# PSUM arrays of one bank each, late exponentials per bank, weight sums after batch 1, earlier attention ranks in a fused attention and MLP kernel

## The chip, the cores and the metric

The kernel runs on one core of a Trainium2 chip. The metric is the device time of one execution in microseconds (us); the time of a kernel is the median of its runs. Before the change it is 321.23 us, the median of three runs (321.04 to 321.79).

The engines are named as in the profile: PE is the matrix engine (PEld its weight loads, which overlap its matmuls), DVE the vector engine, ACT the scalar engine, POOL the GpSimd engine, SP the queue that issues nearly all DMA transfers. Each engine works through its own list of instructions in order; semaphores hold an instruction until what it depends on is done. PE writes its results to PSUM, which has eight banks of 512 fp32 columns on 128 partitions; ACT and DVE read them there.

## The reference

Two stages: windowed attention for eight heads, then an MLP with a leaky ReLU.

```python
# q, k, v: (8 batches, 8 heads, 576 positions, 64), float32
scores = (1 / sqrt(64)) * q @ k.T                        # per batch and head
rel = pos[:, None] - pos[None, :]
mask_plain = (rel >= 0) & (rel < 32)                     # heads 0 to 3
mask_dil = (rel >= 0) & (rel < 128) & (rel % 4 == 0)     # heads 4 to 7
scores = where(mask, scores, -1e9)
attn = exp(scores - max); attn = attn / (sum(attn) + 1e-9)
x = (attn @ v) -> (4608 tokens, 512)                     # heads side by side
h = x @ w_in                                             # 512 -> 2048
g = maximum(0.01 * h, h)
out = g @ w_out                                          # 2048 -> 512, float32
```

## The kernel before

**Work.** Operands are cast to fp16 on the chip. Attention is cut into windows: a block of 96 queries needs 128 keys, and the dilated heads become plain ones when positions are taken modulo 4. Heads go in pairs (`hp`): 0 and 1 are plain (group `g` = 0), 2 and 3 dilated (`g` = 1). Batches 0 and 1 ("early") go through `unit` (L726), three units for each pair, the third one in a second part with its own load (`load_rest`); batches 2 to 7 ("late") go through `late_unit` (L862), two units for each pair, eight for each batch. The attention output is put, transposed, into one of two buffers `xt` (one for each pair of batches). The MLP then works on chunks of 384 tokens, three for each pair of batches, twelve in all: `up` (L994) makes 16 blocks of the hidden layer for a chunk, each four matmuls into a bank `hps` and one ACT eviction with the leaky ReLU into `gt` (L1022). Chunk 0 needs batch 0, chunk 1 batch 1, chunk 2 the rest of both, chunk 3 batch 2, chunk 4 batch 3, chunk 5 the rest of these, and so on (the last three chunks come in the order batch 6, rest, batch 7). The first eight tiles of 128 tokens get their down-projection in the plain way (`down`, L1052: 16 matmuls of 512 columns into a bank `fps`, in four parts, evicted by DVE at L1071 and stored). The other 28 tiles go in groups of four through `group` (L1102), which makes the product of 2 x 2 blocks with seven block products (L1150) in place of eight, and for this needs sums of blocks of `w_out`.

**One attention unit.** The chain is: PE makes transposed q and k for a pair of heads (early: transposes L611 into bank `tpf`, copied out by DVE or ACT at L563 or L561 into `slots`; late: DVE transposes L593 and L604, with POOL's copies L598). PE makes the scores (early L757 or L771, for some units after a bias matmul L754; late L893 or L900). ACT takes the exponential (early L777, late L908). DVE masks (early L791, late L922). PE multiplies with the values, with a column or block of ones for the row sums (early L803, L815, L825, L835; late L929). Early units get the reciprocal on ACT as Ln (L847) and Exp (L849) and are normalised by DVE (L853); late units use DVE's reciprocal (L947) and normalisation (L951), and `across` (L960) transposes the result on PE (L977) and copies it to `xt` (L561 on ACT or L563 on DVE).

**PSUM.** Line 238 makes two arrays of two banks each: `s_two`, with `sps0` (scores of early units) and `tpf` (transposes) as its halves, and `o_two`, with the two `ops` banks as its halves. A late unit writes its scores to both halves of `s_two`, and one exponential of 576 columns reads both. Successive units take the two `ops` banks in turn. `hps0`, `hps1`, `fps0` and `fps1` are arrays of one bank each. In the last group the halves of both arrays serve as four more output banks.

**Weight sums.** `weight_sums` (L1088) makes four DVE instructions of 2048 columns (L1092). Sums 1, 2 and 4 wait for all of `w_out` to be cast, sum 3, written in place, also for the plain down-projections.

**Order.** The order on every engine is fixed when the program is built. `_Plan.run` (L85) goes through all tasks with estimated durations and, where several tasks are ready for an engine, takes the one with the lowest rank (`prio`). The MLP blocks have ranks of `begins[c] + j * 1.3` with `begins` in steps of 20.8 for each chunk. The attention of batch b from 2 on gets ranks from `WHEN[b - 1]` to `WHEN[b]`; batches 0 and 1 have `RANKS`. Loads and casts have ranks from a counter of their own (`tick`), stores come before all. The weight sums have rank `SUMS` = 75. Where the plan leaves PE idle, short matmuls on zeros (L1358) fill in. The plan knows the data and buffer dependencies that the code names; the waits in the program itself come from the accesses to each array and are put in by the framework.

Of the kernel before, what the change touches and what calls it, by code (L numbers as in the profile page):

```python
# [10 lines left out]
FP32 = mybir.dt.float32  # L11
AF = mybir.ActivationFunctionType
# [1 line left out]

WIN = 32
AHEAD, LATE = 5.0, 4.0
WHEN = (-5.0, 15.0, 50.0, 77.0, 112.0, 138.0, 172.0, 200.0)
CON = -1484.5
LOCK = 60.0
AFTER = -1495.0  # L20
# [41 lines left out]
class _Plan:  # L62
# [5 lines left out]
    def add(self, eng, dur, lat, deps, fn, prio, soft=0.0, kind=""):  # L68
        choices = eng if isinstance(eng, tuple) else ((eng, dur),)
        t = _Task(choices, lat, deps, fn, prio, soft, len(self.tasks), kind)  # L70
        self.tasks.append(t)
        return t
# [70 lines left out]
def kernel(  # L143
# [10 lines left out]
    nc = tc.nc  # L154
# [10 lines left out]
    SCALE = float(1.0 / np.sqrt(D))  # L165
# [11 lines left out]
    ps = ctx.enter_context(tc.tile_pool(name="ps", bufs=1, space=bass.MemoryType.PSUM))  # L177
# [4 lines left out]
    def bank(name, dt=FP32):  # L182
        return ps.tile([128, 512 if dt == FP32 else 1024], dt, name=name)

    def at(tl, p0, p1, off, *dims):

        row = tl.ap[0][0]
        return bass.AP(tensor=tl.tensor, offset=tl.offset + p0 * row + off,
                       ap=[[row, p1 - p0]] + [list(d) for d in dims])
# [45 lines left out]
    wide = wst[0].bitcast(FP16)  # L235
    sums = {1: wide[:, 0:2048], 2: wide[:, 2048:4096], 4: t4}

    s_two, o_two = (ps.tile([128, 1024], FP32, name=n) for n in ("sps", "ops"))
    sps0, tpf = s_two[:, 0:512], s_two[:, 512:1024]
    tpb = tpf.bitcast(FP16)  # L240
    ops = [o_two[:, 512 * i:512 * i + 512] for i in range(2)]
    hps = [bank(f"hps{i}") for i in range(2)]
    banks = {"S": [sps0], "O": ops}
    banks["S0"] = banks["S"] + hps[1:]
# [5 lines left out]
    add = plan.add  # L250
# [243 lines left out]
    w_used = [[] for _ in range(16)]  # L494
# [367 lines left out]
    def late_unit(b, g, i, n, prio, turned):  # L862

        dil = g == 1
        hp = 2 * g + i
        ready, t_users, qb, kb = turned[hp]
        _, _, _, vt, v_deps, v_users = visits[b, hp, 0]
        if "S2" not in rings:
            rings["S2"] = [rings["S"][-1] + rings["TP"][-1]]
            o = rings["O"]  # L870
            rings["O2"] = [next(o[-k] for k in (1, 2) if (len(o) - k) % 2 == x) for x in range(2)]
            rings["ED"] = [[] for _ in range(NL)]
            rings["EP"] = [sum(rings["E"][-NE:], [])] * 2
            rings["XN"] = [sum(rings["R"][-NR:], [])] * 2
            rings["REC"] = [[] for _ in range(4)]
        _, s_old = ring("S2", 1, s_users := [])
        en, e_old = ring("ED" if dil else "EP", NL if dil else 2, e_users := [])
        on, o_old = ring("O2", 2, o_users := [])
        cn, c_old = ring("REC", 4, c_users := [])
        if i == 0 and n == 0:  # L880
            xn, x_old = ring("XN", 2, x_users := [])
            xnat[b, g] = x_nat[xn], x_old, x_users, []
        xb, x_old, x_users, made = xnat[b, g]
        et, ot, rt = (el if dil else ee2)[en], ops[on], rec[cn]
        dims = [[192, 2], [336, 2], [1, 144]] if dil else [[1, 576]]
        s_dims = [[512, 2], [144, 2], [1, 144]] if dil else [[512, 2], [1, 288]]

        def scores(e):
            for y in range(2):
                if dil:  # L890
                    c = 2 * n + y
                    for w, k0, c0, x in ((96, 0, 0, 48 * y), (48, 64, 96, 96 * (1 - y))):
                        nc.tensor.matmul(at(s_two, 0, 128, 512 * y + x, [144, 2], [1, w]),  # L893
                                         at(kb, 0, 128, PAD + c + k0, [4, 128]),
                                         at(qb, 0, 128, c * 144 + c0, [S, 2], [1, w]),
                                         start=True, stop=True)
                    continue
                for x in range(3):
                    t = 3 * n + x
                    nc.tensor.matmul(s_two[:, 512 * y + 96 * x:512 * y + 96 * x + 96],  # L900
                                     at(kb, 0, 128, 96 * t, [1, 128]),
                                     at(qb, 0, 128, y * S + 96 * t, [1, 96]),
                                     start=True, stop=True)

        t_s = add("PE", 0.25, 0.25, ready + s_old, scores, prio + 0.1, 0.4, "s")
        t_users.append(t_s)
        t_e = add("ACT", 0.06 + 576 * 0.00085, 0.22, [t_s] + e_old + t_gap,
                  lambda e: nc.scalar.activation(out=at(et, 0, 128, 0, *dims),  # L908
                                                 in_=at(s_two, 0, 128, 0, *s_dims),
                                                 func=AF.Exp, scale=SCALE), prio + 0.1)  # L910
        s_users.append(t_e)

        def mask(e):
            io = [[288, 2], [1, 288]]
            if dil:
                mk, io = at(con, 0, 128, M_DIL, [144, 2], [0, 2], [1, 144]), dims
            elif n == 0:
                mk = at(con, 0, 128, M_PL, [0, 2], [1, 288])
            else:
                mk, io = at(con, 0, 128, M_PL + 96, [0, 6], [1, 96]), [[96, 6], [1, 96]]  # L920
            x = at(et, 0, 128, 0, *io)
            nc.vector.tensor_tensor(out=x, in0=x, in1=mk, op=ALU.mult)  # L922

        t_m = add("DVE", 0.08 + 576 * 0.00056, 0.15, [t_e, t_con], mask, prio + 0.1, 0.0, "M")

        def values(e):
            def one(t, hh, c, k, first, last):
                r = 65 * (2 * t + hh)
                nc.tensor.matmul(ot[:, r:r + 65], et[:, c:c + 128],  # L929
                                 at(vt, 0, 128, (hh * (8 if dil else 6) + k) * 128, [1, 65]),  # L930
                                 start=first, stop=last)
            for t in range(3):
                for hh in range(2):
                    if not dil:
                        one(t, hh, 288 * hh + 96 * t, 3 * n + t, True, True)
                    elif t < 2:
                        one(t, hh, 336 * hh + 240 * t, 2 * n + t, True, True)
                    else:
                        one(t, hh, 336 * hh + 96, 4 + 2 * n, True, False)
                        one(t, hh, 336 * hh + 144, 5 + 2 * n, False, True)  # L940

        t_v = add("PE", 0.23 if dil else 0.17, 0.25, [t_m] + v_deps + o_old, values, prio + 0.2,
                  0.4, "v")
        e_users.append(t_v)
        v_users.append(t_v)
        t_r = add("DVE", 0.13, 0.15, [t_v] + c_old,
                  lambda e: nc.vector.reciprocal(out=rt[0:96, :], in_=at(ot, 0, 96, 64, [65, 6])),  # L947
                  prio + 0.2)

        def norm(e):  # L950
            nc.vector.tensor_tensor(  # L951
                out=at(xb, 0, 96, 768 * n + 64 * i, [256, 3], [128, 2], [1, D]),
                in0=at(ot, 0, 96, 0, [130, 3], [65, 2], [1, D]),
                in1=at(rt, 0, 96, 0, [2, 3], [1, 2], [0, D]), op=ALU.mult)
        t_n = add("DVE", 0.1 + 384 * 0.0011, 0.2, [t_r] + x_old, norm, prio + 0.2)
        o_users.append(t_n)
        c_users.append(t_n)
        made.append(t_n)

    def across(b, g, prio):  # L960
# [3 lines left out]
        for i in range(2):  # L964
# [19 lines left out]
            for c in (chunk_at(m, S * (b % 2)), chunk_at(m, 384)):  # L984
                x_done.setdefault((c, 0), []).append(t_x)

    xnat = {}
    x_nat = [t.bitcast(FP16) for t in rc2]
    t_gap = [clear("POOL", at(t, 0, 128, 144, [336, 2], [1, 48]), 0.15, 0.0, -600) for t in el]
# [90 lines left out]
    def w_block(k, n):  # L1080
        return at(w_out, 0, 128, k * HJ * DM + n * HN, [DM, HJ], [1, HN])

    def flat(tl):
        return at(tl, 0, 128, 0, [HN, HJ], [1, HN])
# [3 lines left out]
    def weight_sums():  # L1088
        w_all = sum((w_out_t[j] for j in range(NJ)), [])

        def minus(n, dst, x, y, deps):
            t_sum[n] = add("DVE", 1.2, 0.2, deps, lambda e: nc.vector.tensor_tensor(  # L1092
                out=dst, in0=x, in1=y, op=ALU.subtract), SUMS, 0.0, "T")
        minus(1, flat(sums[1]), w_block(0, 1), w_block(0, 0), w_all + w_used[9] + w_used[10])
        minus(2, flat(sums[2]), w_block(1, 1), flat(sums[1]), [t_sum[1]])
        minus(4, flat(sums[4]), w_block(1, 0), flat(sums[2]), [t_sum[2]] + rings["VST"][-1])
        minus(3, w_block(0, 1), w_block(1, 1), w_block(0, 1), [t_sum[1]] + plain_parts)
# [265 lines left out]
    for t, u in zip(pe, pe[1:]):  # L1363
# [4 lines left out]
        x = t.start + t.dur + 0.1  # L1368
# [43 lines left out]
```

## Time and profile before

| what | value |
|---|---|
| runs | 321.79, 321.23, 321.04 us |
| the profiled execution's own time | 321.56 us |
| its span, from first to last instruction | 319.8 us |
| busy: PE / PEld / DVE / ACT / POOL | 300.6 / 215.5 / 201.6 / 175.7 / 122.8 us |
| granted PE clock | 1.00 |
| first matmul of chunk 1's up-projection after its wait | 64.88 us |
| weight sums 1, 2 and 4 (L1092) start at | 55.55, 57.88 and 61.62 us, and take 1.22 us each |
| batches 2 to 7: last copy into `xt` ends | 101.8, 130.7, 164.3, 190.1, 234.7, 260.1 us |
| chunks 3, 4, 6, 7, 9, 10 (the first that need these): first eviction starts | 109.3, 131.4, 171.0, 195.5, 245.6, 263.9 us |
| last matmul ends | 315.6 us |

Busy time is the union of an engine's instructions. A matmul's end is modelled: matmuls follow each other faster than their rows are long (a row of 128x384 columns shows 326 ns, eight of them stand in 1.30 us on the chain of waits). So a PE that is busy all the time in this profile may still have short gaps, and idle time in it is surely idle. The two rows on batches and chunks are from the timeline: 24 copies of 576 columns into `xt`, four for each late batch, and sixteen evictions for each chunk (32 in chunk 2, which is cut in halves), counted in order of time.

### The profile page before, as it was taken

The page shows a single profiled execution, that of the slowest core. Times are in us where ns is not written, and L with a number is a line of the kernel's source. Part 1 is how long each engine was busy: PE and PEld are TensorE (multiplying, and loading weights), DVE is VectorE, ACT ScalarE, POOL GpSimd, SP SyncE. Part 2 cuts the span into 40 slices and gives each one's busy share as a digit, 9 for nine tenths or more (in the row PEclk, how much of TensorE's full clock was granted, in tenths as well). Part 3 has the DMA queues.
Part 4 walks back from the last instruction along what each step waited for, and adds up shares of the span by engine and source line. Part 5 has one row for each costly group of instructions (what it writes and reads, how often), then busy time and mean ns, then how long its engine had stood idle before and what let it go on. Part 6 is the DMA issues. An engine that isn't in the chain of part 4 may idle for free.

```text
span 319.8 us, 7327 instructions
## 1 busy us (share of the span) xinstructions
PE 300.6 (94%) x2796; PEld 215.5 (67%) x2796; DVE 201.6 (63%) x421; ACT 175.7 (55%) x376; POOL 122.8 (38%) x178
## 2 busy tenths in 40 slices
PE   7786977899999997999999999999999999999994
PEld 3543643456777765778777877877877777777883
DVE  5754677964774669968989669768744542151342
ACT  3635753586665564645676546466446645455320
POOL 4459554083836457616772955556000000000000
PEclk9999999999999999999999999999999999999999
DMA  7999999699599998697899969794103010210033
GB/s 248 311 336 401 400 306 157 153 229 199 99 238 190 165 230 164 131 188 150 159 210 228 167 138 182 190 187 113 35 10 92 2 33 2 61 49 25 26 107 101
DMA packets 163187, 51.25 MB, mean 160 GB/s; under 512 B 140752, under 2 KB 160080, under 8 KB 163152
## 3 DMA queue, kind: packets, MB, share of 16 engines
q1 hardware_dynamic: 162128, 50.05, 66.0%
q10 hardware_dynamic: 1024, 0.73, 0.8%
q8 instruction: 22, 0.36, 0.5%
q14 instruction: 13, 0.11, 0.1%
HBM read 41.32 MB, written 9.44 MB: 159 GB/s over the span
## 4 chain that ended last, share of the span: by engine, by line
PE 82%; DVE 8%; ACT 5%; issue 1%; DVEq 0%; ACTq 0%
PE hps L1011 36%; PE fps L1150 24%; PE fps L1063 6%; PE ops L929 3%; DVE slots L563 3%; PE ops L977 2%; PE sps L900 2%; PE sps L893 2%; DVE xt L853 1%; ACT ee L777 1%; ACT gt L1022 1%; PE ops L1150 1%; DVE ee L922 1%; ACT rc L847 1%; PE sps L754 1%
## 5 line engine op out<-in xcount | busy, mean ns | idle before, releaser
L1011 PE MATMUL hps<-xt,w_in 128*128 128x384 f16 (+1 forms) x812 | 145.4, 313 | 1.6 <-DVE xt L853 0.6
L1022 ACT ACTIVATE gt<-hps 128x384 f16<-128x384 f32 (+1 forms) x203 | 94.1, 467 | 74.7 <-PE hps L1011 71.6
L1011 PEld LDWEIGHTS <-w_in 128*128 128x128 f16 x832 | 75.9, 98 | 38.0 <-issue 2.0
L1150 PEld LDWEIGHTS <-gt 128*128 128x128 f16 x672 | 64.5, 98 | 11.9
L598 POOL COPY slots<-turned 64x576 f16<-64x576 f16 x48 | 35.9, 747 | 59.5 <-DVE turned L593 48.0
L1150 PE MATMUL fps<-w_out,gt 128*128 128x256 f16 x416 | 53.6, 273 | 0.0
L274 POOL CAST nat<-stg 128x576 f16<-128x576 f32 (+1 forms) x53 | 37.2, 727 | 8.1 <-DMA stg<-in_q_dram 5.2
L1063 PE MATMUL fps<-w_out,gt 128*128 128x512 f16 x128 | 32.7, 379 | 0.2 <-DVE osb L1071 0.2
L1187 DVE TENSOR_TENSOR osb<-fps,stg 128x512 f32<-128x512 f32 x18 | 12.3, 683 | 24.6 <-ACT stg L1179 18.4
L951 DVE TENSOR_TENSOR rc<-ops,recs 96x384 f16<-96x384 f32 x48 | 25.9, 543 | 1.2 <-PE ops L929 0.6
L563 DVE COPY slots<-sps 64x128 f16<-64x128 f16 (+7 forms) x43 | 13.6, 334 | 13.3 <-PE sps L611 6.7
L1179 ACT COPY stg<-fps 128x512 f32<-128x512 f32 (+1 forms) x24 | 12.8, 533 | 14.5 <-PE fps L1150 13.1
L947 DVE RECIPROCAL recs<-ops 96x6 f32<-96x6 f32 x48 | 8.7, 183 | 19.0 <-PE ops L929 18.7
L922 DVE TENSOR_TENSOR ee<-ee,con 128x576 f16<-128x576 f16 x24 | 16.8, 699 | 5.9 <-ACT ee L908 5.6
L274 POOL CAST vd<-v_all 128x1024 f16<-128x1024 f32 (+2 forms) x20 | 17.2, 876 | 6.3 <-DMA v_all<-in_v_dram 5.3
L908 ACT ACTIVATE ee<-sps 128x576 f16<-128x576 f32 x24 | 15.6, 650 | 5.9 <-PE sps L900 5.0
L1063 PEld LDWEIGHTS <-gt 128*128 128x128 f16 x128 | 11.7, 98 | 9.8 <-issue 0.6
L604 DVE STREAM_TRANSPOSE slots<-nat 128x576 f16<-128x576 f16 x24 | 17.8, 748 | 0.6 <-POOL nat L274 0.6
L908 ACT ACTIVATE el<-sps 128x576 f16<-128x576 f32 x24 | 15.6, 650 | 4.5 <-PE sps L893 3.7
L593 DVE STREAM_TRANSPOSE turned<-nat 128x576 f16<-128x576 f16 x24 | 18.0, 755 | 0.0
L922 DVE TENSOR_TENSOR el<-el,con 128x576 f16<-128x576 f16 x24 | 12.8, 535 | 7.6 <-ACT el L908 7.5
L777 ACT ACTIVATE ee<-sps 128x384 f16<-128x384 f32 x20 | 9.8, 490 | 13.0 <-PE sps L771 4.8
(112 smaller groups left out, 378.9 us busy)
## 6 DMA issues: line engine op xcount, KB each, us to landing
stg<-in_q_dram SPq DMA_DIRECT2D x48, 144.0 KB, 3.4
stg<-in_k_dram SPq DMA_DIRECT2D x48, 144.0 KB, 2.9
v_all<-in_v_dram SPq DMA_DIRECT2D x24, 256.0 KB, 4.3
v_all<-in_v_dram SPq DMA_DIRECT2D x24, 192.0 KB, 3.2
gt<-in_moe_w_in_dram SPq DMA_DIRECT2D x5, 512.0 KB, 7.9
out_dram<-osb SPq DMA_DIRECT2D x24, 96.0 KB, 2.0
out_dram<-osb SPq DMA_DIRECT2D x36, 48.0 KB, 1.7
out_dram<-osb SPq DMA_DIRECT2D x25, 64.0 KB, 2.1
```

The source lines that it names most:

```text
L274: ENG[e].tensor_copy(out=dst, in_=src)
L563: nc.vector.tensor_copy(out=dst, in_=src)
L593: lambda e: nc.vector.transpose(xb, na[:, 0:S]), prio)
L598: lambda e, p0=p0, hh=hh: nc.gpsimd.tensor_copy(out=at(qb, p0, p0 + 64, hh * S + o, *od), in_=at(xb, p0, p0 + 64, i, *id_)), prio, 0.0, "m ...
L604: lambda e: nc.vector.transpose(kb[:, PAD:PAD + S], na[:, S:2 * S]), prio)
L908: lambda e: nc.scalar.activation(out=at(et, 0, 128, 0, *dims), in_=at(s_two, 0, 128, 0, *s_dims), func=AF.Exp, scale=SCALE), prio + 0.1)
L922: nc.vector.tensor_tensor(out=x, in0=x, in1=mk, op=ALU.mult)
L951: nc.vector.tensor_tensor(out=at(xb, 0, 96, 768 * n + 64 * i, [256, 3], [128, 2], [1, D]), in0=at(ot, 0, 96, 0, [130, 3], [65, 2], [1, D]) ...
L1011: nc.tensor.matmul(ht[:, 0:n], at(w_in, 0, 128, i * DFF + j // 2 * 256 + j % 2, [2, 128]), at(xt[m % 2], 0, 128, i * 1152 + x0, *dims), st ...
L1022: lambda e: nc.scalar.activation(out=gt[c % NG][:, j * n_c + x:j * n_c + x + n], in_=ht[:, 0:n], func=AF.Prelu, alpha=0.01),
L1063: nc.tensor.matmul(ft, g[:, j * n_c + tt * 128:j * n_c + tt * 128 + 128], w_out[:, j * DM:j * DM + DM], start=(j == 0), stop=(j == NJ - 1))
L1150: nc.tensor.matmul(bk[:, x:x + HN], tl[:, off + j * step:off + j * step + 128], rhs(j), start=first and x == 0 and j == 0, stop=j == HJ - ...
```

## The change

The two arrays of two banks become four arrays of one bank (`bank("sps0")`, `bank("tp")`, `bank("ops0")`, `bank("ops1")`). Since one instruction can no longer read both score banks, a late unit has two exponentials of 288 columns, one for each bank, in place of one of 576, and its mask waits for both. The first weight sum now also waits for the last normalisations of batch 1's second part (`x_done[2, 1]`); sums 2 and 4 follow it. `WHEN`, the ranks of the late batches' attention, gets smaller numbers from its third entry on. Nothing that is computed changes.

```diff
--- before.py
+++ after.py
@@ -14,7 +14,7 @@
 
 WIN = 32
 AHEAD, LATE = 5.0, 4.0
-WHEN = (-5.0, 15.0, 50.0, 77.0, 112.0, 138.0, 172.0, 200.0)
+WHEN = (-5.0, 15.0, 46.0, 70.0, 100.0, 126.0, 160.0, 188.0)
 CON = -1484.5
 LOCK = 60.0
 AFTER = -1495.0
@@ -235,10 +235,9 @@
     wide = wst[0].bitcast(FP16)
     sums = {1: wide[:, 0:2048], 2: wide[:, 2048:4096], 4: t4}
 
-    s_two, o_two = (ps.tile([128, 1024], FP32, name=n) for n in ("sps", "ops"))
-    sps0, tpf = s_two[:, 0:512], s_two[:, 512:1024]
+    sps0, tpf = bank("sps0"), bank("tp")
     tpb = tpf.bitcast(FP16)
-    ops = [o_two[:, 512 * i:512 * i + 512] for i in range(2)]
+    ops = [bank(f"ops{i}") for i in range(2)]
     hps = [bank(f"hps{i}") for i in range(2)]
     banks = {"S": [sps0], "O": ops}
     banks["S0"] = banks["S"] + hps[1:]
@@ -883,32 +882,35 @@
         xb, x_old, x_users, made = xnat[b, g]
         et, ot, rt = (el if dil else ee2)[en], ops[on], rec[cn]
         dims = [[192, 2], [336, 2], [1, 144]] if dil else [[1, 576]]
-        s_dims = [[512, 2], [144, 2], [1, 144]] if dil else [[512, 2], [1, 288]]
 
         def scores(e):
             for y in range(2):
                 if dil:
                     c = 2 * n + y
                     for w, k0, c0, x in ((96, 0, 0, 48 * y), (48, 64, 96, 96 * (1 - y))):
-                        nc.tensor.matmul(at(s_two, 0, 128, 512 * y + x, [144, 2], [1, w]),
+                        nc.tensor.matmul(at(s_two[y], 0, 128, x, [144, 2], [1, w]),
                                          at(kb, 0, 128, PAD + c + k0, [4, 128]),
                                          at(qb, 0, 128, c * 144 + c0, [S, 2], [1, w]),
                                          start=True, stop=True)
                     continue
                 for x in range(3):
                     t = 3 * n + x
-                    nc.tensor.matmul(s_two[:, 512 * y + 96 * x:512 * y + 96 * x + 96],
+                    nc.tensor.matmul(s_two[y][:, 96 * x:96 * x + 96],
                                      at(kb, 0, 128, 96 * t, [1, 128]),
                                      at(qb, 0, 128, y * S + 96 * t, [1, 96]),
                                      start=True, stop=True)
 
         t_s = add("PE", 0.25, 0.25, ready + s_old, scores, prio + 0.1, 0.4, "s")
         t_users.append(t_s)
-        t_e = add("ACT", 0.06 + 576 * 0.00085, 0.22, [t_s] + e_old + t_gap,
-                  lambda e: nc.scalar.activation(out=at(et, 0, 128, 0, *dims),
-                                                 in_=at(s_two, 0, 128, 0, *s_dims),
-                                                 func=AF.Exp, scale=SCALE), prio + 0.1)
-        s_users.append(t_e)
+        t_e = []
+        for y in range(2):
+            def exps(e, y=y):
+                o = (at(et, 0, 128, 192 * y, [336, 2], [1, 144]) if dil
+                     else et[:, 288 * y:288 * y + 288])
+                nc.scalar.activation(out=o, in_=s_two[y][:, 0:288], func=AF.Exp, scale=SCALE)
+            t_e.append(add("ACT", 0.06 + 288 * 0.00085, 0.22, [t_s] + e_old + t_gap, exps,
+                           prio + 0.1))
+        s_users += t_e
 
         def mask(e):
             io = [[288, 2], [1, 288]]
@@ -921,7 +923,7 @@
             x = at(et, 0, 128, 0, *io)
             nc.vector.tensor_tensor(out=x, in0=x, in1=mk, op=ALU.mult)
 
-        t_m = add("DVE", 0.08 + 576 * 0.00056, 0.15, [t_e, t_con], mask, prio + 0.1, 0.0, "M")
+        t_m = add("DVE", 0.08 + 576 * 0.00056, 0.15, t_e + [t_con], mask, prio + 0.1, 0.0, "M")
 
         def values(e):
             def one(t, hh, c, k, first, last):
@@ -984,6 +986,7 @@
             for c in (chunk_at(m, S * (b % 2)), chunk_at(m, 384)):
                 x_done.setdefault((c, 0), []).append(t_x)
 
+    s_two = (sps0, tpf)
     xnat = {}
     x_nat = [t.bitcast(FP16) for t in rc2]
     t_gap = [clear("POOL", at(t, 0, 128, 144, [336, 2], [1, 48]), 0.15, 0.0, -600) for t in el]
@@ -1091,7 +1094,7 @@
         def minus(n, dst, x, y, deps):
             t_sum[n] = add("DVE", 1.2, 0.2, deps, lambda e: nc.vector.tensor_tensor(
                 out=dst, in0=x, in1=y, op=ALU.subtract), SUMS, 0.0, "T")
-        minus(1, flat(sums[1]), w_block(0, 1), w_block(0, 0), w_all + w_used[9] + w_used[10])
+        minus(1, flat(sums[1]), w_block(0, 1), w_block(0, 0), w_all + w_used[9] + w_used[10] + x_done[2, 1])
         minus(2, flat(sums[2]), w_block(1, 1), flat(sums[1]), [t_sum[1]])
         minus(4, flat(sums[4]), w_block(1, 0), flat(sums[2]), [t_sum[2]] + rings["VST"][-1])
         minus(3, w_block(0, 1), w_block(1, 1), w_block(0, 1), [t_sum[1]] + plain_parts)
```

## The prediction

> **What bounds the kernel now.** I read the busy time by stretches first, then the waits and the chain of waits of the stretches where TensorE (PE) is not full, then the timeline there. By stretches, columns being length, PE, PE weight loads, DVE, ACT, POOL, clock, DMA share and GB/s:
>
> ```profile
> 36.00:66.00 30.00, 24.70 (x216) 13.36 (x214) 24.95 (x63) 16.49 (x41) 12.47 (x17) 1.00 0.88 240
> 66.00:120.00 54.00, 53.79 (x538) 37.30 (x537) 34.12 (x74) 35.31 (x83) 29.64 (x40) 1.00 0.95 188
> 120.00:128.00 8.00, 5.89 (x59) 4.38 (x58) 7.43 (x11) 3.81 (x8) 5.78 (x8) 1.00 0.87 165
> 128.00:316.00 188.00, 187.41 (x1772) 144.55 (x1769) 115.06 (x215) 101.70 (x202) 54.65 (x71) 1.00 0.50 108
> ```
>
> From 66 us on PE idles 0.2 us up to 120, 2.1 us from 120 to 128 and 0.6 us up to 316, and the granted clock is full. The change takes no matmul of the projections away, so nearly all that it can win is PE idle time: the 2.1 us, and the 5.3 us (30.00 less 24.70) of 36 to 66, where batch 1's attention has to end before chunk 1's up-projection can start at 64.88. Before 36 us there is more idle time, but the first up-projections wait there for weights: POOL's cast of the fourth w_in tile at 22.59 sat 2.45 us for its DMA, and the DMA share of 20 to 40 us is 1.05.
>
> The timeline of 36 to 66 shows what the waits are (start, length, instruction, idle time before it and what ended it):
>
> ```profile
> 46.39 0.49 ACT L777 ACTIVATE ee<-sps 128x384 f16<-128x384 f32 x1 [0.38 <-DVE slots L563]
> ...
> 46.92 0.41 DVE L563 COPY slots<-sps 64x480 f16<-64x480 f16 x1 [0.56 <-ACT ee L777]
> ...
> 51.62 0.28 PE L815 MATMUL ops<-ee,vd 128*64 128x96 f16 x4 [0.93 <-DVE xt L853]
> ```
>
> The exponential reads bank sps0. The copies of L563 read transposed q and k in the other bank of the same array, tpf. Neither needs the other's data, yet each waits for the other, two reads in turn. L815 likewise writes the ops bank whose last reader ended at 50.43, but starts when the reader of the other ops bank ends, at 51.57. Arrays of one bank don't do this: from 77.72 ACT reads one hps array while PE writes the other without a gap (76.87 to 78.33). So the program orders by array, and the change does what it says.
>
> **Part 1, four arrays.** PE's waits in 36 to 66:
>
> ```profile
> PE ops L815 <- DVE xt L853: 0.9, 1, 0.9
> PE sps L754 <- DVE slots L563: 0.7, 1, 0.7
> PE hps L1011 <- DVE xt L853: 0.6, 1, 0.6
> PE ops L835 <- ACT rc L847: 0.6, 1, 0.6
> PE ops L815 <- ACT rc L847: 0.5, 1, 0.5
> PE ops L835 <- DVE xt L853: 0.5, 1, 0.5
> ```
>
> All but the L1011 row are of the cross-bank kind: 0.9 + 0.7 + 0.6 + 0.5 + 0.5 = 3.2 us. A 384-column matmul has a row of 326 ns but follows its like every 162 ns (8 in 1.30 us), so each gap is understated by some 0.16 us: 5 x 0.16 = 0.8, together 4.0 us. What stands behind them: for the L835 and L815 rows the reader of their own bank had ended 0.5 to 1.2 us before, so these go whole if their other inputs are there; L754 is followed at once by L771, which needs the copies, so that one only shrinks as the copies stop waiting for the exponential (0.61 us at 42.56). PE then reaches the next attention step sooner, and some of those will not be ready. I take a third off: 2.7 us, bounds 1.3 and 6.9 (5.3 plus ten gaps of 0.16, all idle time gone). DVE, at 83% in this stretch, is next in line; without the sums below it has 24.95 less 3.65 = 21.3 us of work there, so it allows 6 us or more.
>
> In 26 to 36 the waits of L757 are 1.1 (on slots) and 0.8 us (on an exponential that had itself sat 2.94 us behind copies of the other bank). But POOL's casts at 35.19 and 36.47 wait 0.77 and 0.67 us for DMA, which sets the pace anew. I take 0.3 us, bounds 0 and 1.9.
>
> In 120 to 128:
>
> ```profile
> 122.11 3.14 DVE L922 TENSOR_TENSOR ee<-ee,con 128x576 f16<-128x576 f16 x1
> ...
> 126.50 0.34 PE L929 MATMUL ops<-vp,ee 128*128 128x65 f16 x6 [2.11 <-DVE rc L951]
> ```
>
> The mask ends at 125.25, its weight load runs at 125.30, but the matmuls wait until 126.46 for the normalisation of the unit before, in the other ops bank: 1.2 us of the 2.1 goes with the arrays. The rest comes from the mask, 3.14 us where its like take 0.46, while POOL casts from 122.68 to 124.94. It stays or goes with the new order: bounds -1.0 (worse) and 2.1, taken 1.2.
>
> **Part 2, the sums behind batch 1.** The chain of waits has two of the three sums on it:
>
> ```profile
> 57.96 0.99 DVE wst L1092
> ...
> 61.62 1.22 DVE v_all L1092
> ```
>
> 2.2 us of chain, but PE had projections to do meanwhile; what it lost is its waits after 59 us: L1011 0.6, L757 0.4 and L825 0.3, all on DVE work queued behind sums. I take 1.3 us, bounds 0.6 and 2.2. The sums issue no DMA. They now follow batch 1's last norms (73.34, two, ended 74.05). Queued behind each on DVE are batch 2's masks and transposes, and PE, POOL and the next copies wait for those: 3 x 1.22 = 3.7 us. The cover is slack: batch 2's last copy into xt ends at 101.8, chunk 3 starts at 109.3, so 7.5 us (3.2 if chunk 3 comes 4.3 us sooner and batch 2 doesn't). Price 0; without the cover 3.7. Their own readers start at 137.7 (L1150 from wst), 60 us later.
>
> [...]
>
> **Part 3, an exponential per bank.** By form:
>
> ```profile
> L908 ACT ACTIVATE ee<-sps 128x576 f16<-128x576 f32 x24 | 15.6, 650 | 5.9 <-PE sps L900 5.0
> ...
> L777 ACT ACTIVATE ee<-sps 128x384 f16<-128x384 f32 x20 | 9.8, 490 | 13.0 <-PE sps L771 4.8
> ```
>
> 160 ns for 192 columns; 288 columns then take 490 - 80 = 410 ns. 48 become 96: 48 x (0.82 - 0.65) = 8.2 us more of ACT rows. Two 192-column ones (0.33 us each) stand in 0.55 us, so a pair overlaps by 0.11 and a unit's mask comes only 0.06 us later. An eviction may now slip between the two (0.49 us later for the mask, sooner for PE). ACT is at 65% in 66 to 120 and 54% later, and PE waited for ACT's evictions 0.3 us in the whole run. Price 0, bounds 0 and 8.2 (each paid by PE).
>
> **Part 4, attention ahead.** WHEN moves the ranks of batches 3 to 7 forward by up to 12, of batch 2's end by 4. Loads and casts are ranked by their own counter, so SP and POOL's casts keep their order; PE and DVE take attention sooner. It matters at one place above all: batch 3's last copy into xt (ACT L561, 130.06 to 130.70, itself 0.51 us behind the DVE copy from the other ops bank) ends after chunk 4's first matmul at 130.49: no slack. Batches 4, 5, 6 and 7 have 6.7, 5.4, 10.9 and 3.8 us. So batch 3 must come sooner by what the start wins, or the win is given back. It was not held by its loads alone: POOL sat 6.9 us for its transposes at 107.46 with the casts done at 101.4. Price 0, bounds -1 and the 4.3 us of the start.
>
> **Sum.** 2.7 + 0.3 + 1.2 + 1.3 = 5.5 us. The profiled execution took 321.56 us (span 319.8 and 1.8 around it), so 316.1; the median is 0.33 lower: 321.2 - 5.5 = 315.7 us.
>
> **Rivals.**
> *Given back at chunk 4.* The start wins 4.3 us, but batch 3's loads (the last issued 99.5 to 102.7, DMA share 0.95 in 66 to 120) don't move, and PE runs dry before chunk 4. Left are 1.2 and the 0.5 of the copy: 319.5. For it: no slack, DMA nearly full. Against: SP stood 6.1 us behind stores of down-projections, which come sooner too. Chance 0.20.
> *More than that.* All idle time of 36 to 66 (6.9), the 2.1 and the 1.9 before 36 go: 10.9, so 310.3. Against: DMA holds the early part, w_out's last cast is at 51.49. Chance 0.15.
> *No effect.* The waits persist for another reason; the sums' 1.3 is lost again in ACT's pairs: 321.2. Against: the hps arrays. Chance 0.05.
> *Slower: attention too far ahead in PE's order.* PE runs in order; where an attention step stands before its mask is done, the projections behind it wait too. DVE was 7 to 9 us busy of every 10 from 120 to 210. One stall of 2.1 us, as at 124, in each of six batches is 12.6, 10.5 more than now; less the start's 4.3 it is 6.2 us slower: 327.4. It decides from the third new stall (2 x 2.1 is about 4.3). For it: that stall. Against: 0.6 us of idle time in 188 us after it. Chance 0.13.
> Forecast: 0.47.
>
> **How the numbers follow.** About 0.2% (0.6 us) is what a measurement of this kernel can tell from no change. Faster: 0.47 + 0.20 + 0.15, and 0.01 of the fourth case: 0.83. Same: 0.04. Slower: 0.13. The range goes from 310.5, near the large case, to 321.0, past the given-back case, and leaves out the slow case, the no-effect case and the end of the large one.
>
> **What would show it.** Right: no wait of L815, L835 or L754 on the other bank's reader; L563's copies and L777 side by side; chunk 1's first matmul near 60.5 instead of 64.88; sums after 70 us at about 1.2 us each; batch 3's last copy before 127; PE idle under 2 us from 66 us to the end. Wrong: chunk 1 early but a gap before chunk 4 (given back); new PE waits on L922 or L951 in several batches (slow); sums of 3 us and batch 2's copies past chunk 3's start.

## The result, and the profile after

The changed kernel took 310.65 us in the median of four runs (309.10 to 311.27), the kernel before 321.51 us beside it (four runs, 321.04 to 322.84): a ratio of 0.9649, 95% interval 0.9599 to 0.9698. The profiled execution took 311.24 us, with a span of 309.5 us against 319.8. The forecast of 315.7 us had the direction; the win was 10.9 us where it had 5.5.

Line numbers moved a little: L1011 is now L1014 (up-projection), L1022 L1025 (its eviction), L563 and L561 L562 and L560 (copies), L777 L776 and L771 L770 (early exponential and scores), L853 L852 (early normalisation), L815 and L825 L814 and L824, L847 and L849 L846 and L848, L908 L910 (late exponential), L922 L924 (its mask), L929 L931, L1092 L1095 (sums), L1136 L1139.

Busy time of the changed kernel by stretches; the columns are those of the same view before (length, PE, PE weight loads, DVE, ACT, POOL, clock, DMA share, GB/s):

```profile
36.00:66.00 30.00, 29.38 (x252) 16.59 (x250) 23.82 (x61) 21.07 (x52) 16.79 (x25) 1.00 0.96 256
66.00:120.00 54.00, 54.00 (x571) 39.33 (x568) 42.05 (x82) 34.96 (x98) 32.96 (x42) 1.00 1.04 207
120.00:128.00 8.00, 8.00 (x83) 5.88 (x82) 7.99 (x15) 6.02 (x15) 5.57 (x6) 1.00 0.77 142
128.00:316.00 188.00, 175.99 (x1656) 135.84 (x1653) 107.26 (x197) 96.68 (x216) 49.58 (x64) 0.99 0.47 103
```

PE's idle time in 36 to 66 went from 5.3 to 0.6 us (fillers are 0.9 us of the busy time), that of 120 to 128 from 2.1 to nothing, and PE now ends at 304 us, so that the last row holds 12 us without matmuls. The waits of PE, first those in 36 to 66, then those from 66 to the end, are one row each:

```profile
PE sps L770 <- DVE slots L562: 0.6, 1, 0.6
```

```profile
PE ops L931 <- DVE ee L924: 0.2, 1, 0.2
```

All rows of these stretches on the reader of another bank are gone. The timeline shows what was two reads in turn (start, length, instruction, idle time before it and its end):

```profile
48.17 0.49 ACT L776 ACTIVATE ee<-sps 128x384 f16<-128x384 f32 x1 [0.93 <-PE sps L770]
...
48.46 1.05 DVE L562 COPY slots<-tp 64x32 f16<-64x32 f16 x3
...
55.61 1.60 PE L1014 MATMUL hps<-xt,w_in 128*128 128x384 f16 x8
```

The exponential reads `sps` until 48.66 while DVE copies out of `tp` from 48.46 on. Chunk 1's matmuls run from 55.61, where those after the wait ran from 64.88.

Three places where the change could have been paid for. First the sums, by line (count, duration in ns, start):

```profile
L1095 DVE TENSOR_TENSOR wst<-w_out x1: 1212/1212/1212, 69.2 to 69.2; 128x2048 f16<-128x2048 f16 x1
L1095 DVE TENSOR_TENSOR wst<-w_out,wst x1: 1225/1225/1225, 70.4 to 70.4; 128x2048 f16<-128x2048 f16 x1
...
L1095 DVE TENSOR_TENSOR v_all<-w_out,wst x1: 1679/1679/1679, 72.4 to 72.4; 128x2048 f16<-128x2048 f16 x1
```

POOL's casts around them, from the timeline:

```profile
67.66 1.28 POOL L273 CAST nat<-stg 128x576 f16<-128x576 f32 x2 [0.72 <-DMA stg<-in_q_dram]
70.56 2.45 POOL L273 CAST nat<-stg 128x576 f16<-128x576 f32 x2 [1.62 <-DMA stg<-in_k_dram]
72.95 1.81 POOL L273 CAST vp<-v_all 128x768 f16<-128x768 f32 x1
...
79.61 0.82 POOL L273 CAST vp<-v_all 128x768 f16<-128x768 f32 x1
```

Then the end of batch 3 and a pair of exponentials:

```profile
117.96 0.46 DVE L562 COPY xt<-ops 128x576 f16<-128x576 f16 x1
118.21 0.64 ACT L560 COPY xt<-ops 128x576 f16<-128x576 f16 x1
118.75 0.42 ACT L910 ACTIVATE el<-sps 128x288 f16<-128x288 f32 x1
...
119.05 0.42 ACT L910 ACTIVATE el<-tp 128x288 f16<-128x288 f32 x1
```

Two sums kept their 1.22 us at the new place, the third lost 0.46 us. The first ran while POOL waited for a DMA. The casts that started behind the second and third (70.56 and 72.95) took longer: 2.45 us for two, where the two at 67.66 took 1.28, and 1.81 us, where the one at 79.61 took 0.82, 2.2 us together. Batch 3's last copy ends at 118.85 and chunk 4's first eviction starts at 120.0: the attention moved with the start. The pair takes 0.72 us (118.75 to 119.47), where one of 576 columns took 0.65.

### The profile page after: what moved, and what is told of

Read it like the earlier page. It is cut to its first block, busy times and chain, and to the rows that moved or that the text cites. A ratio compares the mean times of both kernels' runs of the same rounds, so it can differ in the third digit from the quotient of the medians.

```text
span 309.5 us, 7405 instructions
## 1 busy us (share of the span) xinstructions
PE 297.8 (96%) x2795; PEld 214.1 (69%) x2795; DVE 204.3 (66%) x419; ACT 178.7 (58%) x426; POOL 126.1 (41%) x178
## 4 chain that ended last, share of the span: by engine, by line
PE 87%; DMA 4%; DVE 3%; SPq 3%; ACT 1%; issue 1%; DVEq 0%; ACTq 0%
PE hps L1014 38%; PE fps L1153 25%; PE fps L1066 9%; PE ops L931 3%; DMA wst<-in_moe_w_in_dram 3%; SPq L263 3%; PE ops L979 2%; DVE ee L924 1%; DMA stg<-in_k_dram 1%; PE ops L1153 1%; PE tp L610 1%; PE sps L891 1%; PE tp L891 1%; PE sps L898 1%; PE tp L898 1%; ACT gt L1025 1%
## 5 line engine op out<-in xcount | busy, mean ns | idle before, releaser
L1014 PE MATMUL hps<-xt,w_in 128*128 128x384 f16 (+1 forms) x812 | 144.3, 313 | 1.4 <-DVE w_in L273 0.7
L1025 ACT ACTIVATE gt<-hps 128x384 f16<-128x384 f32 (+1 forms) x203 | 93.7, 468 | 69.9 <-PE hps L1014 67.9
L1014 PEld LDWEIGHTS <-w_in 128*128 128x128 f16 x832 | 75.2, 98 | 37.7 <-DVE w_in L273 1.5
L273 POOL CAST nat<-stg 128x576 f16<-128x576 f32 (+1 forms) x53 | 38.2, 745 | 7.5 <-DMA stg<-in_q_dram 2.7
L273 POOL CAST vd<-v_all 128x1024 f16<-128x1024 f32 (+2 forms) x20 | 18.0, 918 | 5.5 <-DMA v_all<-in_v_dram 5.3
L924 DVE TENSOR_TENSOR ee<-ee,con 128x576 f16<-128x576 f16 x24 | 16.7, 699 | 3.8 <-ACT ee L910 3.7
L562 DVE COPY slots<-tp 64x128 f16<-64x128 f16 (+7 forms) x43 | 13.8, 334 | 8.0 <-PE tp L610 7.4
L924 DVE TENSOR_TENSOR el<-el,con 128x576 f16<-128x576 f16 x24 | 15.7, 656 | 2.1 <-ACT el L910 2.1
L273 POOL CAST vp<-v_all 128x768 f16<-128x768 f32 x16 | 15.4, 970 | 3.3 <-DMA v_all<-in_v_dram 2.1
L1139 DVE TENSOR_TENSOR gt<-gt 128x1024 f16<-128x1024 f16 x19 | 12.9, 692 | 3.8 <-PE fps L1153 3.7
L776 ACT ACTIVATE ee<-sps 128x384 f16<-128x384 f32 x20 | 9.8, 490 | 8.6 <-PE sps L770 5.7
```

The lines of the kernel that those rows point to most:

```text
L273: ENG[e].tensor_copy(out=dst, in_=src)
L562: nc.vector.tensor_copy(out=dst, in_=src)
L1014: nc.tensor.matmul(ht[:, 0:n], at(w_in, 0, 128, i * DFF + j // 2 * 256 + j % 2, [2, 128]), at(xt[m % 2], 0, 128, i * 1152 + x0, *dims), st ...
L1025: lambda e: nc.scalar.activation(out=gt[c % NG][:, j * n_c + x:j * n_c + x + n], in_=ht[:, 0:n], func=AF.Prelu, alpha=0.01),
L1139: lambda e: nc.vector.tensor_tensor(out=dst, in0=a, in1=b, op=op),
```

## The experiments

Each ran beside the kernel before on the same chip. Since the kernels of one study differ in the order of their instructions too, this was compared from the traces: `arrays`, `sps_only` and `exps_only` below have the same order on PE, DVE and ACT (2796 of 2796, 422 of 422 and 423 of 423 records match), and so have `ops_only` and the kernel before (2796 of 2796, 420 of 421 and 376 of 376). Between these a difference is that of the arrays alone, but for spells of half clock (below the table). All other pairs of different kernels differ in order as well.

Three figures per kernel come from its timeline. *Chunk 1* is the start of its first eviction. *Last matmul* is its start. *Idle* is PE's idle time from chunk 1 to the end, worked out by the beat: for each matmul the distance to the next start, less the usual distance for its form (162 ns for 384 columns), summed; this also finds gaps that the modelled ends cover.

| kernel | median us | ratio to before (95%) | chunk 1 | last matmul | idle |
|---|---|---|---|---|---|
| before | 321.5 to 323.2 | 1 | 65.6 | 315.3 | 5.4 |
| changed kernel, again | 310.72 | 0.9624 (0.9587 to 0.9661) | 56.4 | 303.8 | 2.4 |
| arrays | 311.47 | 0.9671 (0.9636 to 0.9705) | 59.3 | 305.1 | 1.7 |
| sps_only | 314.86 | 0.9770 (0.9730 to 0.9809) | 61.8 | 308.5 | 2.5 |
| exps_only | 319.58 | 0.9893 (0.9849 to 0.9938) | 66.0 | 312.5 | 2.2 |
| ops_only | 317.47 | 0.9856 (0.9819 to 0.9893) | 64.5 | 311.3 | 2.6 |
| plan_only | 320.27 | 0.9928 (0.9896 to 0.9960) | 66.1 | 313.2 | 2.9 |
| no_arrays | 323.39 | 1.0031 (1.0001 to 1.0061) | 64.3 | 318.4 | 9.1 |
| sums_only | 325.61 | 1.0096 (1.0059 to 1.0133) | 62.7 | 317.8 | 10.1 |
| when_only | 322.80 | 1.0005 (0.9979 to 1.0031) | 65.6 | 315.2 | 5.3 |
| no_sums | 312.59 | 0.9684 (0.9647 to 0.9721) | 60.0 | 306.3 | 2.1 |
| no_when | 309.76 | 0.9608 (0.9579 to 0.9637) | 56.7 | 304.4 | 2.7 |
| no_fill | 310.29 | 0.9625 (0.9583 to 0.9668) | 56.3 | 304.1 | 2.8 |

Three profiled executions held spells at a granted clock of 0.50 between 24 us and the last matmul, each worth 1.7 us (the last section shows one): `ops_only` one before chunk 1, `sums_only` one after it, `no_arrays` one on each side. Their figures hold these. The medians hold such executions too: of the 52 executions of the kernel before beside these runs, 24 had a mean granted clock of 0.998 or more (median 321.8 us) and 28 one of 0.989 to 0.995 (323.6 us).

**arrays**: the kernel before with the four arrays and the two exponentials, without the sums' move and with the old ranks.

> Before plus part 1 and part 3 only: four arrays of one bank and the exponential per bank; weight sums and ranks as before. Theory A (the waits between the two banks of an array cost far more than the PE waits that the view names, since each also delayed what came behind it on DVE and ACT): 312 to 315 us, chunk 1's up-projection from about 57 to 59 us. Theory B (the waits are worth what was predicted, 2.7 + 0.3 + 1.2, and the rest comes from a better order through the moved sums and ranks): 316 to 318 us, chunk 1 from 61 to 62 us.

This is nearly the whole win: 0.9671 against 0.9649 and 0.9624. Chunk 1 comes 6.3 us sooner, more than the 3.0 predicted for it, and idle time after it falls by 3.7 us. The order differs from that of the kernel before: `exps_only`, below, has the order of `arrays` and 2.8 of its 10.2 us at the last matmul, so 7.4 are the arrays'.

**no_arrays**: only the other two edits.

```diff
-WHEN = (-5.0, 15.0, 50.0, 77.0, 112.0, 138.0, 172.0, 200.0)
+WHEN = (-5.0, 15.0, 46.0, 70.0, 100.0, 126.0, 160.0, 188.0)
...
-        minus(1, flat(sums[1]), w_block(0, 1), w_block(0, 0), w_all + w_used[9] + w_used[10])
+        minus(1, flat(sums[1]), w_block(0, 1), w_block(0, 0), w_all + w_used[9] + w_used[10] + x_done[2, 1])
```

> The changed kernel with the two-bank arrays and the single exponential of before: moved sums and new ranks alone. Theory A: 319 to 321.5 us, chunk 1 from 63 to 65 us. Theory B: 314 to 317 us, chunk 1 from 59 to 61 us.

No gain without the arrays: 0.3% longer, with an interval that begins at 1.0001. Chunk 1 does come sooner (64.3, with 1.7 us of half clock before it). Idle time after it is 3.7 us longer than before, 1.7 of it half clock and 2.0 waits. Without the two spells the last matmul would stand at an estimated 315.0 us (318.4 less 3.4), near the 315.3 of before. PE's waits from 66 us on, its two longest rows:

```profile
PE ops L929 <- DVE rc L951: 2.7, 2, 2.3
PE ops L929 <- DVE recs L947: 0.7, 1, 0.7
```

**ops_only** and **sps_only** split one pair of banks each.

```diff
-    s_two, o_two = (ps.tile([128, 1024], FP32, name=n) for n in ("sps", "ops"))
+    s_two = ps.tile([128, 1024], FP32, name="sps")
-    ops = [o_two[:, 512 * i:512 * i + 512] for i in range(2)]
+    ops = [bank(f"ops{i}") for i in range(2)]
```

> Before with only the two ops banks as two arrays; the score and transpose banks stay one array, one exponential. Same order on all engines as before. Theory A1 (the ops banks carry most: the rows of L815, L835 and the 126.5 us stall are theirs): 315 to 318 us. Theory A2 (the score and transpose banks carry most, since exponentials and copies wait for each other there, in turn): 319 to 321 us.

```diff
-    s_two, o_two = (ps.tile([128, 1024], FP32, name=n) for n in ("sps", "ops"))
-    sps0, tpf = s_two[:, 0:512], s_two[:, 512:1024]
+    o_two = ps.tile([128, 1024], FP32, name="ops")
+    sps0, tpf = bank("sps0"), bank("tp")
...
+    s_two = (sps0, tpf)
```

with two exponentials as in the change.

> Before with only the score bank and the transpose bank as two arrays, and with the exponential per bank; the ops banks stay one array. Theory A1: 319 to 321 us. Theory A2: 314 to 317 us. If the two add up, the gains of this run and of the run with the ops banks alone sum to that of the run with all four arrays; if they stand in one chain, less than the sum appears in each.

Both count. At equal order, `sps` brings chunk 1 from 66.0 (exps_only) to 61.8 and the last matmul from 312.5 to 308.5; `ops` on top of it brings them from 61.8 to 59.3 and from 308.5 to 305.1. By itself, from before, `ops` brings 1.1 us at chunk 1, an estimated 2.8 with the 1.7 us of half clock taken off, so at chunk 1 the two about add up. Together they bring 4.2 + 2.5 = 6.7 us there, and 4.0 + 3.4 = 7.4 us at the end.

Where this is won is read from the same instructions in the three kernels: one group of early values matmuls, then chunk 1's first matmul, each in `exps_only`, `sps_only` and `arrays`.

```profile
36.60 0.36 PE L825 MATMUL ops<-ee,vd 128*128 128x48 f16 x8
34.45 0.36 PE L825 MATMUL ops<-ee,vd 128*128 128x48 f16 x8
34.56 0.36 PE L824 MATMUL ops<-ee,vd 128*128 128x48 f16 x8
...
64.26 0.32 PE L1014 MATMUL hps<-xt,w_in 128*128 128x384 f16 x1
60.09 0.33 PE L1015 MATMUL hps<-xt,w_in 128*128 128x384 f16 x1
57.91 0.32 PE L1014 MATMUL hps<-xt,w_in 128*128 128x384 f16 x1
```

By 36 us `sps` has won 2.15 us and `ops` nothing; from there to chunk 1 `sps` wins 2.0 and `ops` 2.3. PE's wait rows of 36 to 66 gave `ops` 2.5 us, which was near, and `sps` 0.7, which was far too little.

What each leaves is seen in the waits of DVE and ACT in 36 to 66. Of `ops_only`, and then of `sps_only`:

```profile
DVE slots L563 <- ACT ee L777: 5.6, 4, 4.1
```

```profile
ACT rc L847 <- DVE xt L853: 4.5, 4, 1.5
```

In `arrays` neither is left; the longest rows of ACT there are on real data, scores and values:

```profile
ACT ee L776 <- PE sps L770: 3.8, 4, 1.6
ACT rc L846 <- PE ops L802: 3.7, 5, 1.7
```

The stall at 124 is answered by `ops_only`, whose order is that of before. Its timeline:

```profile
120.05 3.15 DVE L922 TENSOR_TENSOR ee<-ee,con 128x576 f16<-128x576 f16 x1
...
123.25 0.35 PE L929 MATMUL ops<-vp,ee 128*128 128x65 f16 x6 [0.92 <-DVE ee L922]
```

The matmuls start as the mask ends (123.20), no longer at the normalisation of the other bank. By the beat the stall fell from 2.27 to 1.08 us, the 1.2 that were predicted; the mask, still 3.15 us long, is what remains.

**exps_only**: two exponentials of 288 columns on the old array of two banks.

```diff
-                                                 in_=at(s_two, 0, 128, 0, *s_dims),
+                nc.scalar.activation(out=o, in_=s_two[:, 512 * y:512 * y + 288], func=AF.Exp, scale=SCALE)
```

> Before with two exponentials of 288 columns in place of one of 576, each on its half of the array of two banks. As predicted (price 0, a pair 0.06 us longer, 8.2 us more of ACT rows): 320.5 to 322.5 us. If ACT's longer pairs hold TensorE: up to 329 us, with waits of the up-projection on ACT.

It was faster, by 1.1%, with more work on ACT. Chunk 1 did not move (66.0); idle time after it fell from 5.4 to 2.2 us. The planner's estimate for an exponential changes with the edit (0.06 us more for the pair), and with it the order on all engines.

**plan_only** keeps the one exponential and changes the estimate alone, so that its order changes and no work does.

```diff
-        t_e = add("ACT", 0.06 + 576 * 0.00085, 0.22, [t_s] + e_old + t_gap,
+        t_e = add("ACT", 0.12 + 576 * 0.00085, 0.22, [t_s] + e_old + t_gap,
```

> Before with nothing changed but the planner's estimate for a late exponential, 0.06 us longer, as that of a pair: one instruction on two banks, another order of the late instructions. Theory G (the 3.4 us that the two exponentials alone won are an order that happens to miss the stall of 2.1 us at 124 us and its like; TensorE's idle time after chunk 1 moves with any change of order while two ops banks share an array): chunk 1 still at 65 to 66 us, a time anywhere from 318 to 325 us, and the difference to before equals the change of the waits of L929. Theory H (shorter ACT instructions win it): 321 to 323 us, the stall at 124 us still there.

0.72% of gain with not one instruction split. Part of this is half clock in the executions of the kernel before: of those with a mean clock of 0.998 or more, five took 321.3 to 322.6 us, and four of `plan_only` 319.0 to 320.5, 0.4% less between the medians. The two profiled executions, both at full clock, differ by 2.1 us at the last matmul. The 2.1 us wait of before is gone; the only row of PE's waits from 66 us on is

```profile
PE ops L929 <- DVE rc L951: 0.3, 1, 0.3
```

So a change of order alone can give most of what `exps_only` won (2.1 of 2.8 us at the last matmul). Its order is not quite that of `exps_only` (388 of 422 DVE records match), and the intervals overlap, so whether the split itself helps by the remaining 0.35% stays open.

**sums_only** and **no_sums**: the sums' move alone (the last two lines of the `no_arrays` diff), and the changed kernel without it.

> Before with only the weight sums moved behind batch 1. As predicted (1.3 us of TensorE's waits after 59 us go): 319.5 to 320.5 us. Theory A (the chain of batch 1 stands on the waits between banks, and new waits of the same kind appear later): 320.5 to 322.5 us, the start of chunk 1 up to 2 us sooner.

> The changed kernel with the weight sums where they were before: arrays, exponentials per bank and new ranks. Theory A (the arrays carry nearly all; once they are in, sums and ranks shift work that TensorE does anyway): within 1 us of the changed kernel, 310 to 312 us, though chunk 1 starts later, near 59 us as with the arrays alone. Theory B (the sums are worth the 1.3 us that was predicted): 311.5 to 313 us, and slower than the changed kernel on the same chip.

Alone the move makes the kernel 1% slower. At chunk 1 it does what it was meant to, 65.6 to 62.7. Then PE stalls. Its waits from 66 us on:

```profile
PE ops L929 <- DVE rc L951: 2.7, 2, 2.6
PE ops L929 <- DVE xt L563: 1.2, 1, 1.2
PE sps L893 <- ACT el L908: 0.7, 1, 0.7
```

These are waits on the arrays of two banks; which of them are on the other bank's reader is not shown. The kernel before had one row, of 2.1 us. Idle time by the beat is 10.1 us against 5.4, 1.7 of it from half clock. With four arrays the same move (no_sums to the changed kernel) takes chunk 1 from 60.0 to 56.4 and the last matmul from 306.3 to 303.8. From arrays to no_when, where the move is added at the old ranks, the gains are 2.6 and 0.8 us. The ratios, 0.9684 to 0.9624 and 0.9671 to 0.9608, say 0.6% both times, with intervals that overlap. So the move is worth some 0.8 to 2.5 us behind the arrays; its exact size is not settled, since the order changes with it.

**when_only** and **no_when**: the first two lines of the `no_arrays` diff alone, and the changed kernel without them.

> Before with only the new ranks. As predicted (price 0): 320.5 to 322 us. Theory F (with two banks in one array, attention ranked ahead puts values matmuls closer behind the normalisation of the unit before, in the other bank of the array, and TensorE waits in order): 322 to 325 us, with more waits of L929 on L951 than the one of 2.1 us.

> The changed kernel with the old ranks: arrays, exponentials per bank and moved sums. Theory A: within 1 us of the changed kernel; batch 3 has come sooner by itself (with the arrays alone its last copy ended at 120.1 us and chunk 4 began at 120.9), so the ranks decide nothing. Theory C (the ranks are needed, since chunk 4 waits for batch 3 once chunk 1 starts at 56.6): 312 to 314 us, with a gap of TensorE of 1 to 3 us before chunk 4.

Nothing either way. With the old ranks batch 3 was done at 120.7 and chunk 4's first eviction started at 121.4 instead of 120.0; the last matmul is at 304.4 against 304.0.

**no_fill** and **after_again**: the changed kernel with the fillers kept to the first 22 us of the plan, and as it is.

```diff
-        while t.start > 0.5 and x + 0.3 < u.start:
+        while 0.5 < t.start < 22 and x + 0.3 < u.start:
```

> The changed kernel without the filling matmuls that the plan puts into its idle time after its 22nd microsecond (ten in the profile of the changed kernel between 24 us and chunk 1, 3.6 us with the waits behind them). Theory D (a filler stands in a gap that is not there on the chip, and delays the attention step behind it): 308.5 to 310 us. Theory E (they fill real waits): 310 to 311 us, no difference, and the granted clock still 1.00.

> The changed kernel itself, for comparison on the same chip: 309 to 311.5 us.

The fillers after 24 us (3.6 us in the changed kernel, with the waits behind them) cost and bring nothing: 0.9625 without them, 0.9624 with them. None of the eleven other kernels is surely faster than the changed kernel; `no_when`, 309.76 us against 310.72, is inside the intervals.

## Why the prediction was right or wrong

**The mechanism** was right: the program orders by array, and with arrays of one bank the waits on the other bank's reader go (before, 3.2 us of PE's rows in 36 to 66; after, the one row there is 0.6 us, on `slots`). All of its signs but one appeared: no wait of L814, L834 or L753 on such a reader, copies beside exponentials, the sums after 69 us, batch 3 done at 118.85 (before 127), no PE wait over 0.2 us from 66 us on. The one is chunk 1, which was to start near 60.5 and started at 55.6.

**Part 1, the start: this step failed, by its size.** "I take a third off: 2.7 us", and "I take 0.3 us" before 36. At equal order the four arrays moved chunk 1's first matmul by 6.35 us (6.7 at its first eviction): 2.0 us before 36 and 4.3 after. The 0.3 was taken since POOL's casts at 35.19 and 36.47 wait for DMA and were to set the pace anew. In `arrays` these casts came no sooner (35.35 and 36.68), but PE did not stand on them: it still led by 2.0 us behind them. The 4.0 us that the 2.7 began from were PE's own wait rows, and the third was taken off since the next attention steps would not be ready. But those steps were late for the same reason. The waits of ACT and DVE in 36 to 66, before:

```profile
ACT rc L847 <- DVE xt L853: 3.6, 4, 1.5
ACT ee L777 <- PE sps L611: 1.7, 2, 0.9
...
DVE slots L563 <- ACT ee L777: 1.9, 3, 0.7
```

Those are 7.2 us of cross-bank waits on the two engines that feed PE, beside 3.2 on PE. That they are cross-bank waits is shown by their going: the first is gone in `ops_only`, the two others in `sps_only`, all three in `arrays`. An attention step is a chain over PE, ACT and DVE; here a wait on any of them delayed the next matmul, where it was entered as a wait for data (or was filled with fillers). The prediction should have walked that chain once without the cross-bank waits, or leaned to its upper bounds, 6.9 and 1.9, of which the second was reached. What it missed most was `sps`: 0.7 us of rows, where it was worth 2.0 in this stretch and another 2.15 before it.

**Part 1, the stall at 124**: 1.2 us predicted and 1.2 measured, in `ops_only`. In the changed kernel the new order had no such stall to save. What was missing is that order alone would save more: `exps_only` and `arrays` lose only 2.2 and 1.7 us of PE time after chunk 1, against 5.4.

**Part 2, the sums**: 1.3 us predicted; 0.8 to 2.5 measured with the arrays, a loss of 1% without them. "Price 0" at the new place held for the changed kernel: batch 2 was done at 95.7 and chunk 3 started at 101.6, so 5.9 us of slack cover the sums. With the arrays of two banks it did not hold (`sums_only`), though the order differs there as well. The sign against it, sums of 3 us, did not come: the second, with casts of POOL beside it from 70.56 on, took 1.23 us, and the third 1.68, where the first took 1.21. The casts beside them took 2.2 us longer and the sums 0.46, so that the three sums took 4.1 us of DVE time. No wait row names these casts, and POOL sat idle from 74.76 to 78.06 behind them.

**Part 3, the exponentials**: the work was right (0.42 us each against 0.41, 0.72 against 0.71 for a pair), and "price 0" was not: 2.8 us of gain at the last matmul in `exps_only`, of which another order alone can give 2.1 (`plan_only`). The bounds, 0 to 8.2, left out a gain.

**Part 4, the ranks**: price 0, and 0 measured, alone and within the change.

**The rivals.** "More than that" (310.3) came nearest: 8.8 us up to chunk 1 and 2.1 after it, against 9.0 measured (chunk 1's first eviction, 65.6 to 56.6) and 2.3 (11.3 at the last matmul, less 9.0); some 2.6 of the 9.0 came with the sums (`arrays` to `no_when`). What spoke against it, DMA, did not hold PE back: in 36 to 66 its share is 0.96, and PE is busy but for 0.6 us. "Given back at chunk 4" did not come: batch 3 moved by 11.9 us, chunk 4 by 11.4, with the old ranks nearly as much. The slower rival's mechanism, a PE queue that stands at an attention step, is what `sums_only` and `no_arrays` show (waits of up to 2.6 and 2.3 us), with arrays of two banks; with four the changed kernel has one such wait of 0.2 us.

## What to carry to other kernels

When two banks lie in one array, add up the cross-bank waits of every engine of the chain, from the start of the program on, not of the one that bounds the kernel: here `sps` had 0.7 us of PE's rows in 36 to 66 and was worth 2.0, since waits of ACT and DVE came back on PE as waits for data. When a planner sets the order, run a variant that changes only an estimate before a gain of a per cent is put down to an edit; and compare kernels of the same order where one is to be had. An edit that frees time early (the sums) may lose it later, where the structure that stalls is still there, so edits are to be tried together as well as alone.

## What the runs showed of the hardware

**Spells of half clock stood behind some stalls.** Busy time of `sums_only` by stretches of 2 us (length, PE, then as above; the third figure from the end is the granted clock):

```profile
126.00:128.00 2.00, 1.08 (x16) 0.82 (x15) 2.00 (x5) 1.38 (x3) 2.00 (x2) 1.00 1.10 234
128.00:130.00 2.00, 0.97 (x10) 0.72 (x11) 1.54 (x5) 0.48 (x1) 2.00 (x3) 0.73 1.06 257
130.00:132.00 2.00, 2.00 (x7) 0.91 (x6) 2.00 (x4) 0.49 (x1) 2.00 (x3) 0.50 0.69 141
132.00:134.00 2.00, 2.00 (x15) 1.48 (x14) 2.00 (x3) 0.59 (x2) 0.56 (x1) 0.92 1.21 191
```

After gaps of 1.95 us together from 126 to 130, the longest of 1.2, the clock is 0.50 for about 3.4 us: 2 x (0.27 + 0.50 + 0.08) = 1.7 us lost. A stall did not always have this behind it. Before, PE was idle 1.6 us of 124 to 126:

```profile
124.00:126.00 2.00, 0.40 (x3) 0.10 (x2) 2.00 (x4) 0.86 (x2) 1.87 (x3) 1.00 1.26 198
```

and the clock stayed full; and the stall of 2.6 us at 151 in `sums_only` left it full, where one of 2.3 us at the same place in `no_arrays` was followed by such a spell. In `no_arrays` chunk 1 came 1.6 us later than in `sums_only`, with a spell at 31 to 35 us in the one and none in the other. Executions of one kernel differ too: 28 of 52 of the kernel before had a mean clock of 0.989 to 0.995, and their median is 1.8 us longer. What sets the spells off was not tried.

**The end of the program varied by 2 us.** The changed kernel's two profiles have their last matmul at 304.0 and 303.8 us and the same order, but spans of 309.5 and 307.4: the stores behind it are issued in 4.80 us by ACT's queue in the one and in 3.44 us in the other. A difference of under 2 us between two single runs of this kernel therefore says nothing of the compute.
